# A state-space and gated feed-forward backward kernel: w1 and w3 are transposed through DRAM during the gradient pass instead of at the start of the input-gradient pass

## The chip, the cores and the metric

The kernel runs on one core of a Trainium2 chip. The metric is the device time of one execution in microseconds (us). Before the change it is 2046.6 us, the median of 7 runs (2042.9 to 2064.46). The core has five engines that work side by side, each through a queue of its own in program order: TensorE (PE, matmuls; PEld are its weight loads), VectorE (DVE), ScalarE (ACT), GpSimd (POOL) and SyncE (SP). SP, ACT and POOL also issue DMA transfers, which 16 DMA engines carry out; SPq and ACTq are these issues in the profile. SBUF is the on-chip memory of 128 partitions, PSUM holds matmul results, DRAM is the memory beside the core.

## The reference, cut to what matters

The forward pass normalizes `u` (2048 x 576), sends it through a diagonal state-space convolution (`_A_ref`, 128 states) and through a gated feed-forward block of width 4608, and multiplies the two. The kernel returns the output and the gradients of `u`, of the eight state-space parameters and of the three weights.

```python
def _B_ref(x, w1, w3, w2):
    gate = jnp.einsum("bsd,df->bsf", x, w1)
    up = jnp.einsum("bsd,df->bsf", x, w3)
    h = _silu(gate) * up
    out = jnp.einsum("bsf,fd->bsd", h, w2)
    return out
...
xn = _layernorm(x, axis=-1)
s = _A_ref(xn, A_A_re, A_A_im, A_B_re, A_B_im, A_C_re, A_C_im, A_log_dt, A_Dskip)
g = _silu(_B_ref(xn, B_w1, B_w3, B_w2))
return x + s * g
```

The part that the change concerns is the gradient of `xn` through the feed-forward block: with GG the gradient of `gate` and GU that of `up` (both 2048 x 4608), it is GG times w1 transposed plus GU times w3 transposed. TensorE needs GG, GU, w1 and w3 with the 4608 axis on the partitions for that, so all four are transposed on the way into SBUF.

## The kernel before, in words

The forward part (lines 86 to 837) ends near 790 us of the span. What follows is `backward`, line 1066, and three strands of work share the engines in it.

**The gradient pass** goes over the 4608 axis in 18 groups of 256 (`FG`). `phase6_load` fetches a group ahead of time: two blocks of w2 through row tiles `w2r` (POOL, line 1139) and transposed on SP into `w2T` (lines 1140 and 1123), the stored gate and up values `gg_n` and `h_n` (POOL, lines 1144 and 1145), and their silu and its derivative (ACT, DVE, lines 1149 to 1154). `phase6_group` computes the gradient of h (matmuls into `ph`, line 1172, from `goT` and `w2T`; ACT casts it to `gh`, line 1175), multiplies it into `gu_n` and `gg_n` (DVE, line 1178), writes these to GU_dram and GG_dram (SP, line 1185), and forms the gradients of w2 (line 1200, from `go_o` and `h_n`) and of w1 and w3 (lines 1219 to 1227, then ACT casts `gw`, lines 1204, 1221 and 1230, and writes on ACT's queue, lines 1205, 1222, 1231 and 1232). `go_o` and the four `goT` tiles stay in SBUF through the pass.

**The state-space gradient** runs beside it: first `conv_bwd_quarter` four times (lines 866 to 948), which ends each quarter by writing 16 pieces of its gradient of `xn` to GXN_dram in fp32 on ACT's queue (line 948), then 36 chunks of `param_quarter` (lines 950 to 980). A chunk loads `gz` (SP, line 959), `qT` by a transposing DMA on SP (lines 962 and 1123) and `pz` (ACT's queue, line 964), multiplies on TensorE into `et_ps` (line 970) and reduces on DVE (lines 977 and 979). The last chunks run beside the next pass; `phase5_final` (lines 982 to 1062) turns their sums into the parameter gradients, with `load_rates` ahead of it.

**The input-gradient pass**, `phase6_inputs`, line 1234, goes over 16 tiles of 128 rows. For a tile, SP loads `ggc` and `guc` (128 x 36 x 128 each) by transposing DMAs from GG_dram and GU_dram (lines 1248 and 1249), with two buffers each; TensorE runs 144 matmuls of 288 columns into `px` (line 1262) over 36 blocks; DVE adds the piece of GXN_dram (`gxs`, line 1255) into `gx` (line 1265), and `ln_bwd_tile` applies the layernorm's gradient and writes `out_1`.

The transposed weights are two sets of tiles. Blocks 0 to 11 of w1 and w3 (`FA = 12`) are loaded by ten transposing DMAs in the gradient pass (line 1097). Blocks 12 to 35 are loaded by ten more in the pool `x_wB`, inside the second pass behind the `ggc` and `guc` of tile 0 (line 1251): the pool lies over the memory of the gradient pass.

The order of each queue is not written out by hand. `self.at(us)` sets the priority of what is traced after it, as a due time (T0 = 560, 36 us for a group, T2 = 1208 for the second pass, 18 us for a tile of it, 15 us for a chunk), and the tile framework orders each engine's instructions by it, allots the slots of each pool and adds the waits. A tile that takes a slot waits for everything that used the slot before. An engine that waits holds all that stands behind in its queue.

Of the kernel before, what the change touches and what calls it, by code (L numbers as in the profile page):

```python
# [11 lines left out]
ALU = mybir.AluOpType  # L12
AX = mybir.AxisListType
FP32 = mybir.dt.float32
BF16 = mybir.dt.bfloat16
I32 = mybir.dt.int32
P = 128
# [43 lines left out]
class K:  # L61
# [669 lines left out]
    def forward_tail(self, T0, TB, TQ, gctx):  # L731
        nc, cfg = self.nc, self.cfg
# [3 lines left out]
        W = D // 4  # L736
# [8 lines left out]
        PS = bass.MemoryType.PSUM  # L745
        gop = gctx.enter_context(pool(name="go_keep", bufs=1))
        self.go_o = gop.tile([P, LT, D], BF16, name="go_o")
# [3 lines left out]
        with pool(name="g_all", bufs=1, side="right") as gp, pool(name="o_ep", bufs=3, side="right") as ep, \  # L751
# [9 lines left out]
            with pool(name="o_ep1", bufs=1) as ep1, pool(name="o_h", bufs=2) as hp, \  # L761
# [41 lines left out]
                for g in range(3):  # L803
                    quarter(g)
            gtp = gctx.enter_context(pool(name="go_t", bufs=1))
            self.goT += [gtp.tile([P, DT, KT * P], BF16, name=f"goT{m}") for m in range(NB // 2, NB)]
# [59 lines left out]
    def conv_bwd_quarter(self, g, kp, zp, ps, T0, TQ):  # L866
# [68 lines left out]
        for j in range(NB):  # L935
# [7 lines left out]
            for oc in range(KT):  # L943
# [3 lines left out]
                nc.vector.tensor_tensor(out=gx[:, oc, :], in0=pt[:, 0:W], in1=gx[:, oc, :], op=ALU.add)  # L947
            nc.scalar.dma_start(out=self.GXN_dram[:, j * KT:(j + 1) * KT, cs], in_=gx[:])

    def param_quarter(self, g, gz, S_all, qp, ps, T0, TC):  # L950
# [3 lines left out]
        for cc in range(NQ):  # L954
# [8 lines left out]
            pz = qp.tile([P, 3, 16, AV], BF16, name="pz")  # L963
            nc.scalar.dma_start(out=pz[:], in_=self.PZ_dram[:, ch])
            for h in range(2):
# [100 lines left out]
    def backward(self, T0, TG, TQ, TC, TX, gctx, mats):  # L1066
# [6 lines left out]
        T2 = T0 + TG * NG  # L1073
        FA = 12
        pool = self.tc.tile_pool
        PS = bass.MemoryType.PSUM
        with ExitStack() as out:
            ffn = ExitStack()
            wp = ffn.enter_context(pool(name="e_w", bufs=2))
            elp = ffn.enter_context(pool(name="e_el", bufs=3))  # L1080
            gwp = ffn.enter_context(pool(name="e_gw", bufs=2))
            rowp = ffn.enter_context(pool(name="e_w2r", bufs=1))
            inp = ffn.enter_context(pool(name="e_in", bufs=2))
            self.at(T0 - TG)
# [11 lines left out]
            self.at(T2 - 150)  # L1096
            wT = [self.load_wT(wA, 0, FA)]
            T1 = T0 + 4 * TQ
# [4 lines left out]
            for gi in range(NG):  # L1103
                nxt = self.phase6_load(gi + 1, T0 + TG * gi, TG, wp, inp) if gi + 1 < NG else None
                self.at(T0 + TG * gi)
                self.phase6_group(gi, cur, elp, gwp, ps_h, ps_gw)
                cur = nxt
            ffn.close()
            gctx.close()
            self.phase6_inputs(T2, TX, FA, wT)  # L1110

    def load_wT(self, pool, f0, f1):
        cfg = self.cfg
        tiles = []
        for w in ("B_w1", "B_w3"):
            t = pool.tile([P, f1 - f0, cfg.D], BF16, name=f"wT{w}{f0}")
            for (do, dsz) in cfg.dch:
                self.nat_transpose(t[:, :, do:do + dsz], self.aps[w][do:do + dsz, f0 * P:f1 * P])
            tiles.append(t)
        return tiles  # L1120

# [3 lines left out]
    def phase6_load(self, gi, T, TG, wp, inp):  # L1125
# [8 lines left out]
        LH = LT // 2  # L1134
        w2T = wp.tile([P, nfl, DT, P], BF16, name="w2T")
        for fl in range(nfl):
            fi = gi * nfl + fl
            w2r = self.w2rows[fi % len(self.w2rows)]
            nc.gpsimd.dma_start(out=w2r[:, 0:D], in_=aps["B_w2"][fi * P:(fi + 1) * P, :])
            self.nat_transpose(w2T[:, fl], w2r[:])  # L1140
        gg = inp.tile([P, LT, FG], BF16, name="gg_n")
        hn = inp.tile([P, LT, FG], BF16, name="h_n")
# [90 lines left out]

    def phase6_inputs(self, T2, TX, FA, wT):
        nc, cfg = self.nc, self.cfg
        D, DT, L, LT, F, FT = cfg.D, cfg.DT, cfg.L, cfg.LT, cfg.F, cfg.FT
        aps = self.aps
        pieces = self.dpieces()
        with self.tc.tile_pool(name="x_wB", bufs=1) as wB, \
                self.tc.tile_pool(name="x_in", bufs=2) as inp, \  # L1240
                self.tc.tile_pool(name="l_sb", bufs=2) as sb, self.tc.tile_pool(name="l_sm", bufs=4) as sm, \
                self.tc.tile_pool(name="x_ps", bufs=2, space=bass.MemoryType.PSUM) as ps:
            for i in range(LT):
                self.at(T2 + TX * i)
                if True:
                    ggc = inp.tile([P, FT, P], BF16, name="ggc")
                    guc = inp.tile([P, FT, P], BF16, name="guc")
                    self.nat_transpose(ggc[:], self.GG_dram[i])
                    self.nat_transpose(guc[:], self.GU_dram[i])
                    if i == 0:  # L1250
                        wT = wT + [self.load_wT(wB, FA, FT)]
                    px = [ps.tile([P, 512], FP32, name=f"px{pi_}") for pi_ in range(len(pieces))]
                    gx = sb.tile([P, D], FP32, name="gx7")
                    gxs = sb.tile([P, D], FP32, name="gxs7")
                    nc.scalar.dma_start(out=gxs[:], in_=self.GXN_dram[:, i, :])
                    go_t = sb.tile([P, D], BF16, name="go7")
                    nc.scalar.dma_start(out=go_t[:], in_=aps["grad_out"].flatten_outer_dims()[i * P:(i + 1) * P, :])
                    for fi in range(FT):
                        part, f = (0, fi) if fi < FA else (1, fi - FA)
                        for ai, act in enumerate((ggc, guc)):  # L1260
                            for pi_, (po, pw) in enumerate(pieces):
                                nc.tensor.matmul(px[pi_][:, 0:pw], lhsT=act[:, fi, :], rhs=wT[part][ai][:, f, po:po + pw],  # L1262
                                                 start=(fi == 0 and ai == 0), stop=(fi == FT - 1 and ai == 1))
                    for pi_, (po, pw) in enumerate(pieces):
                        nc.vector.tensor_tensor(out=gx[:, po:po + pw].rearrange("p (g d) -> p g d", g=4),  # L1265
                                                in0=px[pi_][:, 0:pw].rearrange("p (g d) -> p g d", g=4),
                                                in1=self.perm(gxs[:])[:, :, pi_, :], op=ALU.add)
                    self.ln_bwd_tile(sb, sm, gx, i, go_t)

    def ln_bwd_tile(self, sb, sm, gx, i, go_t):  # L1270
# [8 lines left out]
        nc.scalar.activation(out=t[:], in_=g, func=ACT.Copy, scale=-invD, accum_out=mg[:])  # L1279
        t2 = sb.tile([P, D], BF16, name="t27")  # L1280
        mgx = sm.tile([P, 1], FP32, name="mgx")
        nc.vector.tensor_tensor_reduce(out=t2[:], in0=g, in1=xh, scale=1.0, scalar=0.0, op0=ALU.mult,  # L1282
                                       op1=ALU.add, accum_out=mgx[:])
# [5 lines left out]
        nc.vector.tensor_tensor(out=u[:], in0=g, in1=t[:], op=ALU.add)  # L1289
        o1 = sb.tile([P, D], BF16, name="o1")  # L1290
        nc.vector.scalar_tensor_tensor(out=o1[:], in0=u[:], scalar=self.rstd[:, i:i + 1], in1=go_t[:],
# [96 lines left out]
```

## Time and profile before

| | us |
|---|---|
| median of 7 runs (lowest to highest) | 2046.6 (2042.9 to 2064.46) |
| the profiled execution | 2050.35 |
| its span, first to last instruction | 2048.6 |
| last matmul of the gradient pass starts | 1636.2 |
| first and last matmul of the input-gradient pass start | 1653.1, 2008.7 |
| mean granted TensorE clock, share of full speed | 0.949 |
| transposing DMAs of w1 and w3 on SP: count, median time of one issue | 20, 2.97 |
| transposing DMAs of ggc and of guc: count each, median issue | 16, 5.68 and 6.06 |
| transposing DMAs of qT, of w2T: count each, median issue | 36, 3.70 and 1.23 |

How to read it: a page of the profile gives the busy time of each engine, its share of slices of the span, and groups of instructions by line. A row of a timeline has its start, its length, the engine, the line, the operation, and what it writes and reads (`out<-in`). A wait is named by what ended it. A DMA issue takes time on the queue that issues it, and the data lands later. The DMA share is the mean busy share of the 16 DMA engines; it counts overlapping packets, so it can exceed 1.

### The profile page before, as it was taken

What the parts mean: (1) busy time and instruction counts of PE and PEld (TensorE: products, weight loads), DVE (VectorE), ACT (ScalarE), POOL (GpSimd) and SP (SyncE); (2) the same over time, 40 slices, a digit from 0 to 9 for tenths busy, and PEclk for the clock granted to TensorE, in tenths of its full rate; (3) what the DMA queues carried; (4) which work ended last, traced back from release to release, by engine and by line L of the source; (5) the groups of instructions that cost most, each with busy time, mean ns of one, the idle gap of its engine ahead of it and who ended that gap; (6) DMA issues with size and microseconds to landing.
All of it is one profiled execution on the core that took longest, in us unless ns stands there. A gap on an engine that the chain in (4) does not pass through costs nothing. (4 is left out here: it accounts for less than half of the span.)

```text
span 2048.6 us, 41825 instructions
## 1 busy us (share of the span) xinstructions
PE 1764.7 (86%) x17174; PEld 1292.5 (63%) x17174; DVE 1429.3 (70%) x2772; ACT 992.4 (48%) x1668; POOL 248.6 (12%) x324
## 2 busy tenths in 40 slices
PE   2889999999699995989899998888988938999892
PEld 1534444444488874777777777777777826777681
DVE  7538888888387723685874868666977555768567
ACT  2778888888445545765646656444454200000000
POOL 4003333333312102000000000100000000000000
PEclk9999999999899997999999999999999959999996
DMA  3578888896956568465473655898879499999981
GB/s 84 200 285 305 306 296 300 289 320 250 304 142 175 137 139 263 130 173 168 141 200 113 175 166 157 220 238 212 223 183 218 127 229 215 217 234 196 212 162 22
DMA packets 615087, 416.04 MB, mean 203 GB/s; under 512 B 403184, under 2 KB 560752, under 8 KB 610288
## 3 DMA queue, kind: packets, MB, share of 16 engines
q1 hardware_dynamic: 539632, 264.00, 53.0%
q0 software_dynamic: 23056, 105.00, 14.6%
q10 hardware_dynamic: 52208, 44.37, 8.1%
q8 instruction: 134, 2.20, 0.4%
q14 instruction: 57, 0.47, 0.1%
HBM read 133.01 MB, written 188.01 MB: 157 GB/s over the span
## 5 line engine op out<-in xcount | busy, mean ns | idle before, releaser
L719 PE MATMUL pgu<-wmB_w,xnT 128*128 128x512 bf16 x1152 | 284.1, 382 | 1.1 <-ACT E_k L392 1.1
L1262 PE MATMUL px<-wTB_w,guc 128*128 128x288 bf16 x1152 | 242.4, 291 | 24.2 <-DMA guc<-GU_dram 12.2
L1262 PE MATMUL px<-wTB_w,ggc 128*128 128x288 bf16 x1152 | 244.3, 291 | 20.7 <-DMA ggc<-GG_dram 11.3
L977 DVE TENSOR_TENSOR pr_q<-et_ps,pz 128x512 f32<-128x512 f32 x288 | 186.5, 680 | 92.5 <-PE et_ps L970 92.5
L1219 PEld LDWEIGHTS <-xn_bf 128*128 128x128 bf16 x2304 | 225.0, 98 | 34.5 <-issue 7.6
L1172 PE MATMUL ph<-w2T,goT 128*128 128x256 bf16 x1440 | 194.1, 284 | 32.1 <-ACT gh L1175 30.1
L719 PEld LDWEIGHTS <-xnT 128*128 128x128 bf16 x1152 | 103.5, 98 | 125.2 <-issue 20.9
L1172 PEld LDWEIGHTS <-goT 128*128 128x128 bf16 x1440 | 142.4, 102 | 54.7 <-issue 30.3
L1279 ACT ACTIVATE t<-gx 128x576 f32<-128x576 f32 x16 | 10.9, 683 | 342.1 <-DVE gx L1265 320.6
L979 DVE TENSOR_REDUCE S_all<-pr_q 128x16 f32<-128x1024 f32 x144 | 173.8, 1210 | 0.5
L1200 PE MATMUL pgw<-go_o,h_n 128*128 128x288 bf16 x1152 | 162.2, 296 | 8.4 <-DVE h_n L1154 8.4
L784 PE MATMUL po<-w2g,hc 128*128 128x288 bf16 x1152 | 148.8, 286 | 2.9 <-DMA hc<-H_dram 2.9
L1221 ACT CAST gw<-pgw 128x256 bf16<-128x256 f32 x144 | 54.0, 377 | 199.8 <-PE pgw L1219 195.1
L1262 PEld LDWEIGHTS <-guc 128*128 128x128 bf16 x1152 | 113.8, 99 | 55.6 <-DMA guc<-GU_dram 13.3
L1262 PEld LDWEIGHTS <-ggc 128*128 128x128 bf16 x1152 | 113.3, 99 | 50.4 <-DMA wTB_w<-in_B_w_dram 9.0
L1200 PEld LDWEIGHTS <-h_n 128*128 128x128 bf16 x1152 | 115.4, 101 | 41.3 <-DVE h_n L1154 8.9
L1219 PE MATMUL pgw<-gu_n,xn_bf 128*128 128x256 bf16 x1152 | 131.7, 272 | 3.7 <-ACT gw L1221 1.7
L784 PEld LDWEIGHTS <-hc 128*128 128x128 bf16 x1152 | 111.4, 98 | 30.5 <-DMA hc<-H_dram 3.4
L1219 PE MATMUL pgw<-gg_n,xn_bf 128*128 128x256 bf16 x1152 | 128.9, 273 | 0.8 <-ACT gw L1221 0.8
L1175 ACT CAST gh<-ph 128x512 bf16<-128x512 f32 x144 | 84.3, 618 | 71.3 <-PE ph L1172 34.4
L1178 DVE TENSOR_TENSOR gu_n<-gh,gu_n 128x1024 bf16<-128x1024 bf16 x72 | 49.3, 685 | 97.9 <-ACT gh L1175 97.7
L722 ACT ACTIVATE s_t<-pgu 128x512 bf16<-128x512 f32 x144 | 87.4, 608 | 54.2 <-PE pgu L721 53.9
(301 smaller groups left out, 3622.7 us busy)
## 6 DMA issues: line engine op xcount, KB each, us to landing
GI_dram<-gu_t POOLq DMA_DIRECT2D x72, 512.0 KB, 5.7
H_dram<-h_t SPq DMA_DIRECT2D x72, 256.0 KB, 5.3
Q_dram<-q_k SPq DMA_DIRECT2D x36, 512.0 KB, 5.3
gg_n<-GI_dram POOLq DMA_DIRECT2D x18, 1024.0 KB, 6.0
h_n<-GI_dram POOLq DMA_DIRECT2D x18, 1024.0 KB, 8.8
GU_dram<-gu_n SPq DMA_DIRECT2D x36, 512.0 KB, 3.8
GG_dram<-gg_n SPq DMA_DIRECT2D x36, 512.0 KB, 7.2
E_dram<-E_k SPq DMA_DIRECT2D x18, 768.0 KB, 3.7
```

What stands on the lines that cost most here:

```text
L719: nc.tensor.matmul(pgu[:, j], lhsT=xnT[:, c, ts], rhs=wm[w][:, c, :], start=(c == 0), stop=False)
L722: nc.scalar.activation(out=s_t[:, :, q, :], in_=pgu[:, 0].rearrange("p (g f) -> p g f", g=ng), func=ACT.Silu)
L784: nc.tensor.matmul(pos[k][:, pi_, 0:pw], lhsT=hcs[k][:, fi, :], rhs=w2[fi][:, po:po + pw], start=(fi == 0), stop=(fi == FT - 1))
L977: nc.vector.tensor_tensor(out=pr[:, r], in0=T[r][:], in1=pz[:, s + r, h * 8:h * 8 + 8, :][:, :, None, :] .to_broadcast([P, 8, 2, AV]), op= ...
L979: nc.vector.tensor_reduce(out=S_all[:, 2 * s:2 * s + 2, d0:d0 + 8].rearrange("p k d -> p d k"), in_=pr[:].rearrange("p r d k a -> p d k r ...
L1172: nc.tensor.matmul(ph[j][:, k, :].rearrange("p (a f) -> p a f", f=P), lhsT=lw, rhs=rh, start=(n == 0), stop=(n == nfull))
L1175: nc.scalar.copy(out=gh[:, j], in_=ph[j][:])
L1178: nc.vector.tensor_tensor(out=t_[:, sl], in0=gh[:].rearrange("p j t f -> p (j t) f"), in1=t_[:, sl], op=ALU.mult)
L1200: nc.tensor.matmul(pgw[pi_][:, 0:pw], lhsT=hn[:, tt, fl * P:(fl + 1) * P], rhs=go_o[:, tt, po:po + pw], start=(tt == 0), stop=(tt == LT - 1))
L1219: nc.tensor.matmul(pw_[:, 0:FG], lhsT=self.xn_bf[:, tt, c * P:(c + 1) * P], rhs=nat[:, tt, :], start=(tt == 0), stop=(tt == LT - 1))
L1221: nc.scalar.copy(out=gw[:, c, :], in_=pw_[:, 0:FG])
L1262: nc.tensor.matmul(px[pi_][:, 0:pw], lhsT=act[:, fi, :], rhs=wT[part][ai][:, f, po:po + pw], start=(fi == 0 and ai == 0), stop=(fi == FT - ...
```

## The change

Blocks 12 to 35 of w1 and w3 are transposed three blocks at a time during the gradient pass. For each of groups 0 to 15, `prep_wT` fills a tile by five transposing DMAs on SP and writes it out to a new tensor WT_dram on POOL's queue. The tile takes a slot of `w2T`, whose pool goes from 2 to 3 buffers and whose slots grow to 3 x 576 elements. In the last group `late_wT` loads 20 blocks (10 of each weight) from WT_dram, without transposing, into the `gg_n`, `h_n` and `gu_n` slots that group 16 has left; 16 more go into the four `goT` tiles once the last `ph` matmuls are done, and the last 12 into the pool `x_wB`. All these loads are on SP.

The second pass gets no pool of its own for `ggc` and `guc`. Even tiles use the memory of `go_o`, odd ones the `gg_n`, `gu_n` and `h_n` slots of group 17, where each of the two operands is split into 32 and 4 blocks, so an odd tile has four transposing DMAs. Those of tile 0 are issued before the pass: 34 blocks early, the two of the last group after it.

Besides: GXN_dram is written in the natural order of its columns, so that the add in the second pass reads and writes plain rows in place, by two DMAs on SP in place of one on ACT; `pz` is loaded on SP in place of ACT; two scratch tiles of the layernorm go. The order of the pools changes, since the pool of `gg_n`, `h_n` and `gu_n` must outlive the gradient pass.

```diff
-            nc.scalar.dma_start(out=self.GXN_dram[:, j * KT:(j + 1) * KT, cs], in_=gx[:])
+            for h in range(2):
+                nc.sync.dma_start(out=self.GXN_dram[:, j * KT:(j + 1) * KT, :].rearrange(
+                    "p t (h g d) -> p t h g d", h=2, g=4)[:, :, h, g], in_=gx[:, :, h * W // 2:(h + 1) * W // 2])
...
-            nc.scalar.dma_start(out=pz[:], in_=self.PZ_dram[:, ch])
+            nc.sync.dma_start(out=pz[:], in_=self.PZ_dram[:, ch])
...
-            wp = ffn.enter_context(pool(name="e_w", bufs=2))
+            inp = gctx.enter_context(pool(name="e_in", bufs=2))
             elp = ffn.enter_context(pool(name="e_el", bufs=3))
+            wp = ffn.enter_context(pool(name="e_w", bufs=3))
+            rowp = ffn.enter_context(pool(name="e_w2r", bufs=1))
             gwp = ffn.enter_context(pool(name="e_gw", bufs=2))
-            rowp = ffn.enter_context(pool(name="e_w2r", bufs=1))
-            inp = ffn.enter_context(pool(name="e_in", bufs=2))
...
             self.at(T2 - 150)
-            wT = [self.load_wT(wA, 0, FA)]
+            wT = [[None] * FT, [None] * FT]
+            self.load_wT(wA, 0, FA, wT)
...
+                if gi == NG - 1:
+                    self.at(T0 + TG * gi)
+                    self.late_wT(inp, FA, wT)
...
+    def prep_wT(self, pool, k, FA):
+        cfg = self.cfg
+        FT, D = cfg.FT, cfg.D
+        n = 3
...
+        f, ai = FA + k // 2 * n, k % 2
+        if f >= FT:
+            return
+        t = pool.tile([P, n, D], BF16, name="w2T")
+        for (do, dsz) in cfg.dch:
+            self.nat_transpose(t[:, :, do:do + dsz],
+                               self.aps[("B_w1", "B_w3")[ai]][do:do + dsz, f * P:(f + n) * P])
+        self.nc.gpsimd.dma_start(out=self.WT_dram[ai, :, f:f + n, :], in_=t[:])
+
+    def wT_into(self, dst, ai, f0, wT):
+        n = dst.shape[1]
+        if f0 == 0:
+            for (do, dsz) in self.cfg.dch:
+                self.nat_transpose(dst[:, :, do:do + dsz], self.aps[("B_w1", "B_w3")[ai]][do:do + dsz, 0:n * P])
+        else:
+            self.nc.sync.dma_start(out=dst, in_=self.WT_dram[ai, :, f0:f0 + n, :])
+        for f in range(n):
+            wT[ai][f0 + f] = dst[:, f, :]
...
+        self.at(T + 0.5 * TG)
+        self.prep_wT(wp, gi, self.FA)
+        self.at(T)
...
+            self.at(T2 - 0.5 * TG)
+            gts = []
+            for m in range(4):
+                t = (self.gop if m < 2 else self.gtp).tile([P, DT, self.cfg.KT * P], BF16, name=f"goT{m}")
+                n = DT * self.cfg.KT * P // D
+                gts.append(t[:].rearrange("p c t -> p (c t)")[:, 0:n * D].rearrange("p (r d) -> p r d", d=D))
+            for ai in range(2):
+                for j in range(2):
+                    self.wT_into(gts[2 * ai + j], ai, self.fl + n * j, wT)
...
+            sets = [[[(0, FT, even[:, ai])] for ai in range(2)],
+                    [[(0, FL, odd[ai]), (FL, FT, odd[2][:, ai * (FT - FL):(ai + 1) * (FT - FL)])] for ai in range(2)]]
+            FN = FT - self.FG // P
+            for ai, src in enumerate((self.GG_dram, self.GU_dram)):
+                self.nat_transpose(even[:, ai, 0:FN], src[0, :, 0:FN * P])
+            self.load_wT(wB, fl, FT, wT)
+            self.at(T2 - 0.3 * TG)
+            for ai, src in enumerate((self.GG_dram, self.GU_dram)):
+                self.nat_transpose(even[:, ai, FN:FT], src[0, :, FN * P:FT * P])
...
-                    ggc = inp.tile([P, FT, P], BF16, name="ggc")
-                    guc = inp.tile([P, FT, P], BF16, name="guc")
-                    self.nat_transpose(ggc[:], self.GG_dram[i])
-                    self.nat_transpose(guc[:], self.GU_dram[i])
-                    if i == 0:
-                        wT = wT + [self.load_wT(wB, FA, FT)]
+                    parts = sets[i % 2]
+                    if i > 0:
+                        for ai, src in enumerate((self.GG_dram, self.GU_dram)):
+                            for (a, b, t) in parts[ai]:
+                                self.nat_transpose(t[:, 0:b - a], src[i, :, a * P:b * P])
...
-                        nc.vector.tensor_tensor(out=gx[:, po:po + pw].rearrange("p (g d) -> p g d", g=4),
-                                                in0=px[pi_][:, 0:pw].rearrange("p (g d) -> p g d", g=4),
-                                                in1=self.perm(gxs[:])[:, :, pi_, :], op=ALU.add)
-                    self.ln_bwd_tile(sb, sm, gx, i, go_t)
+                        nc.vector.tensor_tensor(out=gxs[:, po:po + pw], in0=px[pi_][:, 0:pw], in1=gxs[:, po:po + pw],
+                                                op=ALU.add)
+                    self.ln_bwd_tile(sb, sm, gxs, i, go_t)
```

## The prediction

> **What bounds the kernel now.** I read the busy shares first, then the slices, then the stretch where the slices of TensorE dip, and there the queue of SyncE (SP), which issues every transposing DMA. The first line says that TensorE is the busiest engine over the whole span; the three stretches under it (start:end, length, busy us of each engine, then granted clock, DMA share, GB/s) say that one stretch is different.
>
> ```profile
> PE 1764.7 (86%) x17174; PEld 1292.5 (63%) x17174; DVE 1429.3 (70%) x2772; ACT 992.4 (48%) x1668; POOL 248.6 (12%) x324
> ```
> ```profile
> 1590.00:1637.00 47.00, 46.88 (x492) 40.51 (x490) 24.52 (x36) 11.93 (x29) 0.00 (x0) 1.00 0.45 127
> 1637.00:1712.00 75.00, 31.47 (x259) 22.16 (x259) 36.70 (x51) 0.78 (x2) 0.00 (x0) 0.66 1.12 222
> 1712.00:1769.00 57.00, 56.84 (x537) 45.32 (x536) 33.42 (x54) 2.33 (x6) 0.00 (x0) 1.00 1.14 221
> ```
>
> In the last gradient group (to 1637) TensorE is full and the DMA engines are less than half used; then for 75 us TensorE works 31.5 us, at a granted clock of 0.66, while the DMA share stands at 1.12; after that TensorE is full again, with the DMA share no lower. The SP timeline says what fills the gap:
>
> ```profile
> 1642.37 5.67 SPq L1123 DMA_TRANSPOSE ggc<-GG_dram  x1
> 1648.09 6.26 SPq L1123 DMA_TRANSPOSE guc<-GU_dram  x1
> 1654.40 35.15 SPq L1123 DMA_TRANSPOSE wTB_w<-in_B_w_dram  x10
> ...
> 1693.08 4.91 SPq L1123 DMA_TRANSPOSE ggc<-GG_dram  x1
> 1698.03 5.57 SPq L1123 DMA_TRANSPOSE guc<-GU_dram  x1
> ```
>
> Ten transposes of w1 and w3 (two thirds of them, 2x576x3072x2 B = 7.08 MB) take SP 35.15 us, 201 GB/s, ahead of tile 1's own transposes. Nothing before 1637 covers them. Tile 0's result is taken from PSUM at 1701.6, tile 1's at 1727.9, and tile 13's at 1970.0 (starts of the L1265 rows): 242.1/12 = 20.2 us a tile in the steady pass.
>
> **Part 1, the ten transposes leave the second pass.** TensorE's account: tile 0 needs go_o free (last L1200 matmul ends 1620.1), so its transposes can enter SP behind the last group's GU/GG writes (issued to 1621.3). Two big ones at the medians 5.7 us issue and 10 us to landing: 1621.3+5.7+10 = 1637. The last two blocks wait for the last GG write (1620+7.2) and then for the big ones on SP; by the small w2T transposes (1.23 us issue, 2.6 us landing) 1633+2.5+2.6 = 1638. Six plain loads (four into the goT tiles, two into wB) may stand ahead or behind at 0.5 us each. So tile 0 can begin near 1641 instead of ending at 1701.6; one steady tile of 18.8 us (spacing of tiles 1 to 3) ends at 1660, 42 us earlier. Tile 1 came 26.3 us after tile 0 and would come 20.2 after: 6 us more. **Saving by TensorE: 48 us.** Behind tile 13 the tail (SP loads the rates behind the last guc, then phase5_final on DVE, then tile 15's layernorm, 78.6 us from 1970.0 to the end) keeps its order and shifts with it.
>
> The DMA engines' account is smaller. The 7.08 MB do not vanish from this stretch: they come back as plain loads, late_wT 2.95 MB in the last group, goT 2.36 and wB 1.77 MB at the boundary. At the best slice of the page, 320 GB/s, they take 22 us, at 222 GB/s 32 us; take 24, so 35-24 = 11 us are saved. The rest must come from the unused DMA of the last group: from 1602, when the tiles of group 16 are free, to 1637 the share is 0.53 against 1.12, (1.12-0.53)/1.12 x 35 = 18 us. **Saving by DMA: 30 us.** Which one counts depends on whether the pass is bound by TensorE or by DMA, and it is nearly both: a tile asks for 4.4 MB (ggc and guc 2.36, 1.2 chunks of qT, pz and gz at 1.18, gxs, go and o 0.59), at 221 GB/s 19.7 us, between the 18.8 of a full TensorE and the 20.2 on average. I take the middle, **39 us**, ends 30 and 48.
>
> **Part 2, the toll in the gradient pass (790 to 1637).** Added: 16 blocks of 5 transposes on SP, 16 writes of 442 KB on POOL. Nearest row from below: the 36 small w2T transposes held TensorE for 2.0 us in all (its waits), 0.056 us each, 80 x 0.056 = 4.5 us. Nearest row from above, the first third of w1 and w3, ten transposes in the same pass:
>
> ```profile
> 1309.00:1362.00 53.00, 41.27 (x410) 34.40 (x408) 28.57 (x44) 19.83 (x33) 6.92 (x7) 0.92 1.11 252
> ```
>
> TensorE is at 41.3 of 53 us where the rest of the stage has 89% (290.7 of 327): 5.8 us lost for 3.54 MB, so 12 us for 7.08 MB. DMA has room: the share is 0.58 from 790 to 1310, which leaves 251 us of full use; transposes 32 us plus the extra write and its load. SP itself: 5 x 1.23 = 6.2 us a group of 47 us, with waits of tens of us in it now. A prep tile takes the slot of the group's own w2T, so it waits for the last ph matmul (L1172), as the next w2T does today (126.4 us of SP waiting); behind it stand the GU/GG writes, qT and gz. The WT_dram write on POOL waits for its transposes; behind it stand w2r, gg_n and h_n of a later group, which today wait for the end of L1227 anyway. **I take 8 us**, the middle of 4.5 and 12.
>
> **Part 3, the moves between queues.** GXN writes: 16 of ACT become 32 on SP with pieces of 288 B instead of 576. DVE waits for them today 12.3 us in 4 waits (gx L941); doubled, +12.3; below, 0; I take 3, since most are not waited for. pz goes from ACT to SP, 36 x 0.33 us; in front of ACT's casts stand waits for DVE that fit it (gh after pr_q and S_all, 3.8+2.4 us), so up to -6 us, and on SP pz waits for DVE with ggc behind it; I take -2 in the gradient pass. The odd tiles' splits are 2 more small transposes in 8 tiles, 2 x 1.23 x 8 = 20 us of SP, hidden while DMA and not SP is the limit; without that cover half of it would be late. The add in natural order and o1 as scratch replace rows of 0.45 and 0.74 us by equal ones: 0. Toll of parts 2 and 3: 8+3-2 = 9 us, ends -30 (all the time that TensorE's ph waits for gh goes) and +86 (below).
>
> A rule against part 3: the Trainium skill, "DMA: Bandwidth & Descriptors", Specifications, wants at least 512 B per piece for full rate, and 288 B lies below it where 576 did not. The trace shows 576 B pieces landing in 3.0 us (median); no run here shows 288 B. If each of 16 landings doubled by that rule and DVE waited for all, the sum would be 48 us worse; by the trace's own waits it is the 0 to 12 above.
> A second: the same page, Rules for kernel authors, calls transfers under 64 KB mostly overhead. The 64-row pieces here are 48 KB, the others 96 KB; the smallest transposes of the trace are the 160 KB w2T. If these 80 paid 2 us each by that rule, SP would carry 160 us more over 16 groups, still inside its waits.
>
> **Sum.** Profiled execution: span 2048.6, time 2050.35, so 1.75 us lie around it; it is 3.75 us over the median of the seven runs, 2046.6, and I carry the difference over. -39+9 = -30: 2050.35-30 = 2020.4, and against the median 2046.6-30 = **2016.6 us**.
>
> **Rivals.**
> *DMA keeps all of it* (chance 0.2): the pass is DMA-bound throughout, the saving is 30, the toll at 12+12 = 24: -6, **2040.6**. For: share 1.14 to 1.19 to the end, late guc at 1902 and 1974. Against: TensorE 56.84 of 57 us.
> *TensorE's account is right and the queues get lighter* (0.2): -48 and the toll 0 or below: -48 to -62, **1998** or less. For: the waits on ACT that may go.
> *ACT is held by SP's transposes, slower* (0.13). Writes on ACT's queue were held until a transpose on SP landed:
> ```profile
> ACT gh L1175 <- DMA qT<-Q_dram: 16.2, 3, 8.3
> ```
> (gh's waits: total, times, longest), 5.4 us each; at 1576.31 the write of gw2 goes out as qT lands, 15.9 us after its issue. If each of 16 prep blocks does it once, 16 x 5.4 = 86 us and the sum is -39+86 = +47, **2094**; it decides from 39/16 = 2.4 us per block. Half of it, +4, is 2051. Against: small transposes land in 2.6 us, qT in 6.2.
> *The gap stays* (0.07): tile 0's transposes are queued behind late loads and the stall takes another name: **2046**.
>
> Chances: forecast 0.4 (2005 to 2030). Range: 0.1 off each end, 1990 to 2052. A measurement here tells about 0.5%, 10 us, from no change: faster 0.4+0.2+0.07 (a third of the first rival) = 0.67, same 0.20, slower 0.13.
>
> **What would show it.** Right: TensorE at 90% or more from 1637 on, clock 1.0 instead of 0.66; no wB transposes between tiles 0 and 1; the first DVE reads of px, against the end of the gradient pass, about 42 us earlier for tile 0 and 30 to 48 for tile 13; DMA share in the last group near 1; gradient pass 0 to 20 us longer. Part 2 wrong: waits of gh or gw for a DMA of w2T (the prep tiles), or of ph for gh, well over 30 us. Part 1 wrong: a new wait of px for goT, wB or ggc, or tiles over 21 us apart.

## The result and the profile after

The changed kernel takes **2080.97 us**, the median of 12 runs (2063.02 to 2091.5), against 2046.93 for the kernel before beside it (31 runs): a ratio of **1.0151, 95% interval 1.0126 to 1.0176**. It is slower by 34 us where 30 us less was forecast. Its profiled execution took 2076.51 us with a span of 2074.7; the kernel before had 2050.35 and 2048.6, so the two traces differ by 26.1 us in the span.

Where the 26.1 us lie is read from one row, the last `gwt` cast of ACT, which ends the gradient pass: 1636.53 before, 1710.70 after. **The gradient pass ends 74.2 us later; what follows it is 48.1 us shorter** (412.1 us before, 364.0 after). Stretches of the profile after (start:end, length, busy us of PE, PEld, DVE, ACT, POOL, then granted clock, DMA share, GB/s); the first is the end of the gradient pass, the other two begin where it ends:

```profile
1680.00:1710.70 30.70, 30.62 (x302) 26.33 (x300) 14.20 (x21) 7.84 (x19) 0.00 (x0) 1.00 1.11 288
1710.70:1785.70 75.00, 60.42 (x574) 46.64 (x574) 53.97 (x76) 1.92 (x5) 0.00 (x0) 0.93 1.14 240
1785.70:1842.70 57.00, 55.63 (x544) 43.68 (x542) 47.67 (x72) 2.33 (x6) 0.00 (x0) 1.00 1.14 230
```

The gap is gone: in the 75 us where TensorE worked 31.5 us at a clock of 0.66 it now works 60.4 at 0.93. The toll is in the pass ahead of it. The same stretch in both kernels, from 790 us to the end of the pass, before and after:

```profile
790.00:1636.53 846.53, 750.88 (x7650) 636.45 (x7651) 603.76 (x1095) 457.04 (x949) 42.46 (x72) 0.96 0.68 183
```
```profile
790.00:1710.70 920.70, 776.09 (x7690) 652.59 (x7688) 609.02 (x1104) 461.56 (x956) 50.86 (x86) 0.93 0.72 189
```

TensorE does the same work: 750.9 x 0.96 = 721 against 776.1 x 0.93 = 722. So 25 us of the 74 are longer matmuls at a lower granted clock and 49 us are idle time. Group by group (the `gwt` cast of each of the 18) the lag grows: 17 us at group 0, 27 at group 1, 32 at group 4, 46 at group 9, 80 at group 13, and 74 at the end. The waits say what holds it. ACT waiting for gg_n between 780 and 1720 us (total, times, longest), before and then after:

```profile
ACT gu_n L1149 <- DMA gg_n<-GI_dram: 9.1, 6, 2.3
ACT L1149 <- DMA gg_n<-GI_dram: 1.0, 2, 0.7
```
```profile
ACT L1193 <- DMA gg_n<-GI_dram: 76.3, 11, 13.1
ACT gu_n L1193 <- DMA gg_n<-GI_dram: 1.2, 1, 1.2
PE ph L1216 <- ACT gh L1219: 60.2, 20, 8.9
```

ACT's wait for gg_n went from 10.1 us to 77.5, and TensorE's own wait for `gh`, which ACT casts, went from 30.1 to 60.2. One group shows how. The timelines of POOL, SP and ACT of the kernel after, around the end of a group at 1494.72:

```profile
1493.87 0.55 POOL L1137 DMA_DIRECT2D WT_dram<-w2T  x1 [14.75 <-DMA w2T<-in_B_w_dram]
1501.16 0.54 POOL L1180 DMA_DIRECT2D w2r<-in_B_w_dram  x1 [6.74 <-DMA w2T<-w2r]
1502.47 0.54 POOL L1180 DMA_DIRECT2D w2r<-in_B_w_dram  x1 [0.76 <-DMA w2T<-w2r]
1503.05 0.54 POOL L1188 DMA_DIRECT2D gg_n<-GI_dram  x1
```
```profile
1482.14 9.79 SPq L1163 DMA_TRANSPOSE w2T<-in_B_w_dram  x3
1498.02 2.52 SPq L1163 DMA_TRANSPOSE w2T<-w2r  x2
```
```profile
1494.72 0.37 ACT L1274 CAST gwt<-pgw 128x256 bf16<-128x256 f32 x1 [1.53 <-PE pgw L1271]
1497.77 0.58 ACT L1219 CAST gh<-ph 128x512 bf16<-128x512 f32 x1 [0.34 <-PE ph L1216]
1511.44 1.28 ACT L1193 ACT_TABLE_LOAD   x1 [13.09 <-DMA gg_n<-GI_dram]
```
```profile
1514.31 1.65 PE L1216 MATMUL ph<-w2T,goT 128*128 128x256 bf16 x7 [8.88 <-ACT gh L1219]
```

The buffer of gg_n is free when the group ends, 1494.72. But POOL stands first before the write of the prep block (its transposes took 9.79 us for three of the five issues), then before two `w2r` loads, whose row tiles the `w2T` transposes must have read; these in turn stand on SP until the block's write has freed their slot. gg_n goes out at 1503.05, ACT's silu starts at 1511.44, and ACT does nothing for 13.09 us while TensorE waits 8.88 us for the `gh` behind it. Before, POOL stood at gg_n itself and let it go as the group ended at 1477.00; the `w2r` ahead of it had gone out 20 us earlier:

```profile
1477.23 0.53 POOL L1144 DMA_DIRECT2D gg_n<-GI_dram  x1 [19.41 <-PE pgw L1227]
1496.18 0.53 POOL L1145 DMA_DIRECT2D h_n<-GI_dram  x1 [18.42 <-PE pgw L1200]
```

### The profile page after: what moved, and what is told of

The parts are those of the page before. It is cut to its first block, busy times and chain, and to the rows that moved or that the text cites. A ratio compares the mean times of both kernels' runs of the same rounds, so it can differ in the third digit from the quotient of the medians.

```text
span 2074.7 us, 42081 instructions
## 1 busy us (share of the span) xinstructions
PE 1782.1 (86%) x17174; PEld 1303.2 (63%) x17174; DVE 1429.2 (69%) x2772; ACT 992.3 (48%) x1668; POOL 264.5 (13%) x340
## 5 line engine op out<-in xcount | busy, mean ns | idle before, releaser
L1216 PE MATMUL ph<-w2T,goT 128*128 128x256 bf16 x1440 | 200.8, 290 | 62.9 <-ACT gh L1219 60.2
L784 PE MATMUL po<-w2g,hc 128*128 128x288 bf16 x1152 | 153.9, 292 | 16.2 <-DMA hc<-H_dram 16.2
L1343 ACT ACTIVATE t<-gxs 128x576 f32<-128x576 f32 x16 | 10.9, 683 | 296.6 <-DVE gxs L1330 296.6
L1327 PEld LDWEIGHTS <-go_o 128*128 128x128 bf16 x1152 | 111.8, 99 | 38.4 <-DMA go_o<-GU_dram 6.4
L582 PEld LDWEIGHTS <-dSi 128*128 128x128 bf16 x768 | 76.4, 100 | 41.9 <-issue 41.0
L467 DVE TENSOR_SCALAR m_k<-et_ps 128x512 int32<-128x512 int32 x108 | 73.7, 682 | 33.0 <-PE et_ps L466 32.7
L728 POOL DMA_DIRECT2D GI_dram<-gu_t x72 | 68.5, 952 | 216.3 <-DVE gu_t L724 110.2
```

The source lines that it names most:

```text
L467: nc.vector.tensor_scalar(out=m[:, o:o + 512], in0=pt[:].bitcast(I32), scalar1=15, scalar2=15, op0=ALU.logical_shift_left, op1=ALU.arith_s ...
L582: nc.tensor.matmul(pv, lhsT=mat[:, kt, sl], rhs=V[:, :, ri, kt, :], start=(i == 0), stop=(i == n - 1))
L784: nc.tensor.matmul(pos[k][:, pi_, 0:pw], lhsT=hcs[k][:, fi, :], rhs=w2[fi][:, po:po + pw], start=(fi == 0), stop=(fi == FT - 1))
L1216: nc.tensor.matmul(ph[j][:, k, :].rearrange("p (a f) -> p a f", f=P), lhsT=lw, rhs=rh, start=(n == 0), stop=(n == nfull))
L1327: nc.tensor.matmul(px[pi_][:, 0:pw], lhsT=act, rhs=wT[ai][fi][:, po:po + pw], start=(fi == 0 and ai == 0), stop=(fi == FT - 1 and ai == 1))
```

## The experiments

Ratios are to the kernel before, run on the same chip in the same session, with 95% intervals. Runs of one kernel scatter by 10 to 30 us, so differences under some 8 us between medians are not told apart. Theory A: the toll is the prep blocks, through the order of the queues. Rival C: it is the transfers moved between queues. A second rival, B, came up on the way: it is the DMA work of the blocks, their traffic or the transposes as such.

**No blocks at all.** Left out: the 16 blocks; the late loads read rows of w2, so the gradient of `u` is another.

```diff
-        self.at(T + 0.5 * TG)
-        self.prep_wT(wp, gi, self.FA)
-        self.at(T)
...
-            self.nc.sync.dma_start(out=dst, in_=self.WT_dram[ai, :, f0:f0 + n, :])
+            self.nc.sync.dma_start(out=dst, in_=self.aps["B_w2"][f0 * P:(f0 + n) * P, :].rearrange("(r p) d -> p r d", p=P))
```

> The change without its prep blocks: no transposes of w1 and w3 in the groups and no writes to the scratch tensor; the late loads read rows of w2 of the same shape instead, so the input gradient is computed from w2 in place of blocks 12 to 35 of w1 and w3. Everything else stays: pool order, three w2T buffers, GXN writes and pz on SP, the second pass without transposed weights. Theory A (the toll is the prep blocks): the gradient pass, which ends at 1636.5 us before and 1710.7 after, ends at 1635 to 1655, and the time is 1998 to 2020. Theory C (the toll is the reordering of the pass by the moved GXN and pz transfers and the pools): the pass still ends past 1690 and the time is 2055 or more.

Measured: 2004.26 us, ratio 0.9778 (0.9718 to 0.9838). The stretch from 790 us to the end of the pass is 4.5 us longer than before, and ACT waits 11.4 us for gg_n:

```profile
790.00:1641.03 851.03, 754.11 (x7665) 639.10 (x7665) 607.26 (x1103) 459.73 (x956) 41.86 (x71) 0.96 0.70 191
```

What follows the pass takes 364.5 us, as in the changed kernel. So everything else that the change does is worth 43 us, and the blocks cost 2081 - 2004 = **77 us**. Rival C is out. Against the kernel before this pass is 12.6 us late at group 0 and 4.5 at its end, so the lag that grows through the pass comes from the blocks.

**Transposes without the writes.** The WT_dram write is left out too, the blocks are transposed and not kept.

```diff
-        self.nc.gpsimd.dma_start(out=self.WT_dram[ai, :, f:f + n, :], in_=t[:])
```

> As the first, but the 80 small transposes stay and only the 16 writes on POOL's queue go; the late loads again read w2, so the input gradient is computed from w2 in place of blocks 12 to 35 of w1 and w3. Theory A1 (POOL's write, which waits for its transposes, holds back the next group's gg_n load, ACT stands before silu with the gh casts behind it): ACT's wait for gg_n falls from 76 us to under 20, the pass ends at 1640 to 1665, time 2000 to 2030. Theory B (the transposes themselves, by SP's queue and the DMA engines): the pass ends past 1690, time 2055 or more.

Measured: 2048.81 us, 1.0017 (0.9984 to 1.005), between the two ranges: ACT still waits 32.1 us for gg_n and the pass ends at 1681.9. Taken in this order, the transposes bring 45 of the 77 us and the writes on top of them 32. With no write in its queue POOL still has `w2r` ahead of gg_n; the last cast of the group starts at 1481.89:

```profile
1482.29 0.54 POOL L1179 DMA_DIRECT2D w2r<-in_B_w_dram  x1 [17.53 <-DMA w2T<-w2r]
1485.24 0.54 POOL L1179 DMA_DIRECT2D w2r<-in_B_w_dram  x1 [2.41 <-DMA w2T<-w2r]
1485.83 0.53 POOL L1187 DMA_DIRECT2D gg_n<-GI_dram  x1
```

**The write on SP instead of POOL.**

```diff
-        self.nc.gpsimd.dma_start(out=self.WT_dram[ai, :, f:f + n, :], in_=t[:])
+        self.nc.sync.dma_start(out=self.WT_dram[ai, :, f:f + n, :], in_=t[:])
```

> The change with the 16 writes to the scratch tensor issued on SP instead of POOL; TensorE's and ACT's orders are the same as in the change. On POOL the next gg_n then stands behind two w2r loads only, which wait for w2T. Theory A1 in its short form (the write alone): ACT's wait for gg_n under 25 us, the pass ends at 1650 to 1675, time 2015 to 2040. Theory A2 (the chain write, w2T slot, w2r, gg_n): w2T still takes the slot that the write frees, so only part comes back: the pass ends at 1680 to 1705, time 2045 to 2070. Theory B: 2075 or more, since SP has more to do.

Measured: 2074.09 us, 1.0132 (1.0075 to 1.019), not told apart from the changed kernel. The ranges of A1 and A2 are both missed, and it is 1 us short of that of theory B. ACT's wait for gg_n falls from 77.5 to 47.2 us, yet the pass ends at 1710.2 as in the changed kernel. So the write's place on POOL was not the toll by itself; that the wait only moved to SP's queue is the reading, and it is not shown.

**gg_n on ACT's queue.**

```diff
-        nc.gpsimd.dma_start(out=gg[:], in_=self.GI_dram[gi, :, 0])
+        nc.scalar.dma_start(out=gg[:], in_=self.GI_dram[gi, :, 0])
```

> The change with one line altered: the 18 loads of gg_n are issued on ACT's queue, so nothing of POOL stands ahead of them. Theory A1 or A2: the loads go out within 1 us of the group's end, ACT's wait for gg_n falls under 30 us, the pass ends at 1650 to 1680 and the time is 2015 to 2045. Theory B: no change, 2070 or more.

Measured: 2040.82 us, 0.9948 (0.9908 to 0.9989). **One line gives 40 of the 77 us back.** ACT's own queue reaches the load as the group ends, so nothing that is due earlier stands behind it; the wait for gg_n is 17.2 us in the pass:

```profile
1480.56 0.34 ACTq L1188 DMA_DIRECT2D gg_n<-GI_dram  x1
1480.94 0.37 ACT L1274 CAST gwt<-pgw 128x256 bf16<-128x256 f32 x1 [1.88 <-PE et_ps L972]
...
1486.53 1.28 ACT L1193 ACT_TABLE_LOAD   x1 [0.22 <-DMA gg_n<-GI_dram]
```

**The side moves alone**: the kernel before with GXN's writes and pz on SP (the first two parts of the diff of the change) and the add in natural order.

```diff
-                        nc.vector.tensor_tensor(out=gx[:, po:po + pw].rearrange("p (g d) -> p g d", g=4),
-                                                in0=px[pi_][:, 0:pw].rearrange("p (g d) -> p g d", g=4),
-                                                in1=self.perm(gxs[:])[:, :, pi_, :], op=ALU.add)
+                        nc.vector.tensor_tensor(out=gx[:, po:po + pw], in0=px[pi_][:, 0:pw], in1=gxs[:, po:po + pw],
+                                                op=ALU.add)
```

> The kernel before with only the side moves: each GXN write as two on SP with half-length pieces, pz on SP, the add of the second pass in natural order. Theory A (the toll comes from the prep blocks, in the queues): these moves are cheap, about the 4.5 us by which the gradient pass of the kernel without preps was longer; 2042 to 2056 us, point 2050. Rival C (the moved transfers are the toll): 2075 or more, with DVE waiting for gx or PE for qT over 30 us more than before.

Measured: 2023.38 us, 0.9881 (0.9845 to 0.9917). Neither theory had this: the moves do not cost, they give 24 us. Two runs later split it (below).

**The blocks two loads later**: none is issued ahead of the forward's last `hc` transposes.

```diff
-        self.prep_wT(wp, gi, self.FA)
+        self.prep_wT(wp, gi - 2, self.FA)
...
-        if f >= FT:
+        if k < 0 or f >= FT:
```

> The changed kernel, but the first prep block is issued with the load of group 2 instead of group 0, so that no prep block stands in SP's queue ahead of the hc transposes of the forward's end; the last of the 16 goes out with the load of group 17. POOL's order (w2r, w2r, gg_n) stays. Theory A: only the early part of the toll comes back, that is the 12 us by which group 0 to 4 of the changed kernel lie behind those of the kernel without preps; 2062 to 2074 us, point 2068, and ACT still waits 60 us or more for gg_n. If the early blocks cost nothing: 2081. If the whole toll came from them: below 2040.

Measured: 2073.55 us, 1.014 (1.0079 to 1.0201). Group 0's lag falls from 16.8 to 6.8 us and group 9's from 46.1 to 34.5, but at the end it is 69.2 against 74.2, which the scatter covers; ACT waits 81.4 us for gg_n, both inside what theory A expected. The early blocks are not the toll.

**Both edits, and with h_n on ACT as well**, two kernels; the second has this line more:

```diff
-        nc.gpsimd.dma_start(out=hn[:], in_=self.GI_dram[gi, :, 1])
+        nc.scalar.dma_start(out=hn[:], in_=self.GI_dram[gi, :, 1])
```

> Both edits: gg_n's load on ACT's queue and the prep blocks two loads later. Theory A (queue order): the two costs lie in different places, so both come back; 2040.8 less 8 to 16, 2025 to 2033 us, point 2029; group 0 ends 10 us or more earlier than with gg_n on ACT alone. Rival B (what is left of the toll is DMA traffic: 21 MB more in the pass, TensorE's clock): the place of the blocks does not matter, 2036 to 2044.

> As the one before, and h_n's load on ACT's queue too, so that POOL issues only w2r and the writes of the transposed blocks, and nothing that the gradient group reads waits behind them. Theory A: up to the 14 us that TensorE still waited for h_n with gg_n alone on ACT, and no more: 0 to 10 us under the run before it, 2018 to 2030, point 2024. Rival B: no gain, within 3 us of it; slower than it if ACT now waits for h_n's buffer ahead of its casts.

Measured: 2041.34 us, 0.9968 (0.9935 to 1.0), and 2046.21 us, 1.0 (0.9966 to 1.0034). Theory A failed here twice: the first result is in rival B's range, the second 5 us slower still, which the scatter covers. The two edits do not add up, and taking the last load of a group off POOL gives nothing: ACT's wait for gg_n is 9.3 and 8.0 us, as before the change, yet 37 us of the toll stay (2041 - 2004, medians). The first kernel's trace is of its fastest execution, 2026.34 us, 19 above that of the kernel without blocks, so its waits show only about half of these 37. With h_n on ACT TensorE waits 24.9 us for ACT's `gw` casts instead.

**What the 37 us hang on.** Three kernels, each that with gg_n on ACT and late blocks and one more edit. The first leaves out the write (the late loads read w2). The second keeps the write and fills a block by one plain load of w2 rows, so its second pass has other numbers:

```diff
-        for (do, dsz) in cfg.dch:
-            self.nat_transpose(t[:, :, do:do + dsz],
-                               self.aps[("B_w1", "B_w3")[ai]][do:do + dsz, f * P:(f + n) * P])
+        self.nc.sync.dma_start(out=t[:], in_=self.aps["B_w2"][f * P:(f + n) * P, :].rearrange("(r p) d -> p r d", p=P))
```

The third does the whole work, with the blocks in a buffer of their own, each released behind the first quarter silu of a load; gg_n is on ACT from group 2 on:

```diff
-            wp = ffn.enter_context(pool(name="e_w", bufs=3))
+            wp = ffn.enter_context(pool(name="e_w", bufs=2))
+            pp = self.prepp = ffn.enter_context(pool(name="e_p", bufs=1))
...
-        t = pool.tile([P, n, D], BF16, name="w2T")
+        t = pool.tile([P, n, D], BF16, name="w13T")
+        self.nc.scalar.copy(out=t[0:1, 0, 0:D:P], in_=after[0:1, 0, 0:5])
...
             nc.scalar.activation(out=gu[:, sl, :], in_=gg[:, sl, :], func=ACT.Silu)
+        if gi >= 2:
+            self.prep_wT(self.prepp, gi - 2, self.FA, gu)
```

> Measured so far: 2004 us with no prep blocks, 2041 with gg_n on ACT and the blocks two loads later; 37 us of toll are still open. This kernel is the latter without the writes of the blocks; the transposes stay, and the late loads read rows of w2 instead, so the two gradients that the second pass makes are not the reference's. Theory S (what is left is the slot chain: w2T and prep tiles alternate in three buffers, and SP stands before a buffer): a buffer is free as soon as its transposes have landed, so most of it goes: 2008 to 2025 us, point 2018. Theory B (what is left is the transposes' own DMA work): 2034 to 2044.

> gg_n on ACT, blocks two loads later, writes kept, but each block is brought in by one plain load of w2 rows (442 KB) instead of five transposes, so the second pass computes with other numbers than the reference. The buffers and the waits for them stay. Theory S: the chain is the same, 2034 to 2044 us. Theory B (transposing costs, not the bytes): the toll goes, 2005 to 2020. Point 2030.

> The whole work, with the prep blocks in a buffer of their own (w2T has its two again), each block's transposes released by a five-element copy on ACT behind the first quarter silu of the load, first block with the load of group 2, gg_n on ACT from group 2 on. Theory S: SP never stands before a buffer that TensorE or the block's write holds: 2006 to 2022 us, point 2015, under the 2023 of the moves alone. Theory B: 2034 to 2044.

Measured: without the write 2017.55 us, 0.9834 (0.9784 to 0.9885); plain load 2001.38, 0.9754 (0.9709 to 0.9798); own buffer 2020.97, 0.9858 (0.9801 to 0.9914). So 24, 40 and 20 of the 37 us go. Theory B is wrong in the first and third run, theory S in the second: the slots count (own buffer), and the transposes count although slots and writes stay (plain load). The third run changes three things at once, though: the blocks' buffer, the two slots of `w2T` and the moment a block is released. The plain load moves the same 442 KB (the DMA share of the pass is 0.76 in both), so it is not the bytes. The pass in the kernel with transposes and in that with plain loads:

```profile
790.00:1661.26 871.26, 752.31 (x7652) 638.31 (x7651) 609.08 (x1102) 457.37 (x953) 39.99 (x67) 0.94 0.76 202
```
```profile
790.00:1630.17 840.17, 745.80 (x7643) 633.90 (x7643) 606.00 (x1099) 458.33 (x954) 40.03 (x67) 0.96 0.76 208
```

What differs is the time that a block holds SP and its buffer: five issues of 1.25 us (median; up to 6.8) and 2.7 us to landing, against one of 0.39 (up to 3.6) and 3.5. The chain is slot, transposes, landing, write, slot, `w2T`: whole it costs 37 us, some 13 to 17 without the write or with a slot of its own, and nothing when its longest link, the transposes, is short. That reading fits the three runs, but it is argued: no single wait of TensorE carries the 37 us.

**Own buffer, gg_n left on POOL**, and the same with the write on SP behind the group's GU/GG writes:

```diff
-        self.nc.gpsimd.dma_start(out=self.WT_dram[ai, :, f:f + n, :], in_=t[:])
+        self.pend = (self.WT_dram[ai, :, f:f + n, :], t)
...
                 nc.sync.dma_start(out=dst[ts, :, gi * FG:(gi + 1) * FG].rearrange("t p f -> p t f"), in_=t_[:, ts, :])
+        if self.pend:
+            nc.sync.dma_start(out=self.pend[0], in_=self.pend[1][:])
+            self.pend = None
```

> As the run before it, but gg_n stays on POOL, where it is now again ahead of the two w2r of its load as in the kernel before. Theory A with S (what hurt was gg_n behind w2r, w2T and their buffers): within 10 us of the run before it, 2008 to 2030, ACT waits for gg_n under 25 us. If any wait of POOL for a block's transposes hurts gg_n: 2050 or more, with 50 us of ACT waiting for gg_n.

> The whole work, blocks in a buffer of their own and released as in the two runs with that, gg_n on POOL, and the block's write on SP behind the group's GU/GG writes, so that POOL issues w2r, gg_n and h_n alone, as in the kernel before. If POOL's wait for the block was what lay between 2021 (gg_n on ACT) and 2034 (on POOL): 2010 to 2024 us, point 2018. If SP's wait for the landing costs as much: 2030 to 2040.

Measured: 2034.42 us, 0.9918 (0.9879 to 0.9957), and 2037.86 us, 0.9945 (0.9914 to 0.9976). The first is above its range, though ACT's wait for gg_n, 22.5 us, is as expected; the second is in the range of the alternative. In the second POOL issues nothing of the blocks, and ACT still waits 46.2 us for gg_n. In the two longest of its seven waits, 27.5 us of the 46.2, a `w2r` ahead of gg_n has waited for `w2T` on SP, where a block and its write stand ahead. In one of them, with the group's last cast at 1416.01:

```profile
1409.71 2.81 SPq L1232 DMA_DIRECT2D WT_dram<-w13T  x1
1412.58 6.10 SPq L1166 DMA_TRANSPOSE w2T<-w2r  x1
```
```profile
1424.37 0.54 POOL L1182 DMA_DIRECT2D w2r<-in_B_w_dram  x1 [16.07 <-DMA w2T<-w2r]
1424.98 0.54 POOL L1187 DMA_DIRECT2D gg_n<-GI_dram  x1
```
```profile
1432.56 1.28 ACT L1192 ACT_TABLE_LOAD   x1 [12.63 <-DMA gg_n<-GI_dram]
```
```profile
ACT L1192 <- DMA gg_n<-GI_dram: 46.2, 7, 14.9
```

In the longest wait, 14.9 us, gg_n went out only 3 us after the group's last cast, and the load itself took 15.5 us to land.

**Plain loads in the changed kernel itself**, gg_n on POOL, everything else as changed.

> The changed kernel with one edit: each block comes in by one plain load of w2 rows instead of five transposes, so the second pass computes with other numbers than the reference. gg_n on POOL, the three shared buffers, the order of issue by the same rule and the write stay. If gg_n's place behind w2r and the buffers costs by itself: 2030 to 2045 us, with 50 us or more of ACT waiting for gg_n. If the chain only costs through the length of the transposes (6 us of SP for a block, then the landing): 2000 to 2012, gg_n waits near 10. Point 2010.

Measured: 2028.15 us, 0.9922 (0.9884 to 0.996), between the two theories, with ACT waiting 30.1 us for gg_n. With it the toll can be laid out in a square (medians; no blocks: 2004; the 2001 has its blocks two loads later, which made no difference to the 2041):

| | gg_n on POOL | gg_n on ACT |
|---|---|---|
| transposed blocks | 2081 | 2041 |
| plain blocks | 2028 | 2001 |

gg_n's place costs 27 us without the transposes and 40 with them; the transposes cost 40 us without gg_n's place and 53 with it. So the shares depend on the order in which they are taken: the blocks with gg_n on POOL cost 24 us even when nothing is transposed.

**pz alone, and GXN with the add alone**, each on the kernel before; the first is this line, the second the rest of the side moves.

```diff
-            nc.scalar.dma_start(out=pz[:], in_=self.PZ_dram[:, ch])
+            nc.sync.dma_start(out=pz[:], in_=self.PZ_dram[:, ch])
```

> The kernel before with pz's load on SP instead of ACT, nothing else. If the 24 us of the side moves come from ACT no longer standing before pz's buffer with its casts behind it: 2020 to 2030 us, point 2025. If they come from GXN's writes and the add: 2042 to 2050.

> The kernel before with GXN's writes as two half-length pieces on SP and the add in natural order; pz stays on ACT. If pz is the cause: 2040 to 2050 us. If GXN is: 2022 to 2030. By the prediction's own term it would lose 3: 2050.

Measured: pz 2025.98 us, **0.9906 (0.9868 to 0.9944)**; GXN and the add 2054.03 us, 1.0013 (0.9977 to 1.0048). pz is the cause: 19 us by the ratio. A place where the two kernels differ is ACT's timeline in the kernel before, at group 16: `gw` is cast, its write issues 9 us later, as a transpose of qT on SP ends, and `gh` behind it is as late.

```profile
1566.84 0.68 ACT L1204 CAST gw<-pgw 128x288 bf16<-128x288 f32 x2
1567.40 1.07 ACT L1149 ACTIVATE gu_n<-gg_n 128x1024 bf16<-128x1024 bf16 x1
1576.31 0.38 ACTq L1205 DMA_DIRECT2D out_dram<-gw  x1
1576.73 1.07 ACT L1175 CAST gh<-ph 128x512 bf16<-128x512 f32 x2 [8.26 <-DMA qT<-Q_dram]
```
```profile
1567.38 8.89 SPq L1123 DMA_TRANSPOSE qT<-Q_dram  x1
```

With pz on SP the write follows the cast at once; the three waits of `gh` for qT (16.2 us in all) are gone in that kernel and in that with all the moves, and 11.1 us of them stay where only GXN was moved. No load of pz issues on ACT between 1562.32 and 1576.31, so how its place there holds a later write is not shown:

```profile
1567.59 0.68 ACT L1204 CAST gw<-pgw 128x288 bf16<-128x288 f32 x2
1568.16 1.07 ACT L1151 ACTIVATE gg_n<-gg_n 128x1024 bf16<-128x1024 bf16 x1
1568.30 0.35 ACTq L1205 DMA_DIRECT2D out_dram<-gw  x1
```

The kernels that do the whole work and are fastest are the own buffer with gg_n on ACT (2021), the moves alone (2023) and pz alone (2026); the runs do not tell them apart.

## Why the prediction was wrong, point by point

**The failed step** is this one of part 2: "The WT_dram write on POOL waits for its transposes; behind it stand w2r, gg_n and h_n of a later group, which today wait for the end of L1227 anyway." It took for granted that gg_n would still be issued when L1227 ends. In the trace of before only gg_n waits for that; the `w2r` wait for `w2T` on SP, and had gone out 11 to 26 us before the group's end. With the blocks SP is late with `w2T`, the second `w2r` goes out after the group's end in 11 of 13 groups, and gg_n goes out 3 to 11 us after it in 10 of 16. The step beside it, "SP itself: 5 x 1.23 = 6.2 us a group of 47 us, with waits of tens of us in it now", failed too, since SP's waits were not free time: what stood behind them came late. **Toll of part 2: 8 taken, 4.5 to 12 as the ends, 77 measured.** The upper end came from ten transposes whose results nothing in the pass waits for, so it priced their DMA and not their place in a queue. (Its 89% also counted the slow 53 us themselves; the other 275 us are at 91%, which makes it 14 instead of 12.)

**Part 1** was right for the second pass, and short of an entry for the first. What follows the gradient pass is 48.1 us shorter, TensorE's account (48); the first read of px comes 37.1 us after the end of the pass instead of 65.1, so 28 earlier and not 42, and tile 13 at 1998.65, 45.4 us earlier, inside the 30 to 48. The rest is the tail. Two corrections: about 10 us of this stretch came with the side moves alone (401.9 us after the pass against 412.1, one trace each), and the kernel without blocks has a gradient pass 14.6 us longer than that with the moves alone (1641.0 against 1626.4), an entry that the sum did not have. By medians the step from the moves alone to no blocks is worth 19 us (2023 to 2004), where 39 was taken. Of these 14.6 us, 6.5 are there at group 0, where six `w2T` transposes that the third buffer lets go early stand ahead of four `hc` transposes (TensorE waits 11.3 us for hc, against 1.1 with the moves alone).

**Part 3**: GXN +3, pz -2, add 0, so +1 was taken; measured -24 (pz 19, GXN and add nothing that can be told). The "up to -6 us" was read from waits of `gh` for DVE (pr_q and S_all), and these stayed with pz on SP: 7.1 us in place of 6.2. What went are the 16.2 us of `gh` waiting for qT, which the prediction showed in a fence for another purpose. The rule on pieces under 512 B that was weighed there would have made it 48 us worse; with GXN moved alone the half-length pieces of 288 B landed in 2.8 us (median; 4.3 in the changed kernel) against 3.0 for the whole ones, and that kernel is at 1.0013. The 2 us for each small transfer were counted as time of SP; the 80 transposes issue in 1.25 us (median), and only the 16 of 48 KB are under the 64 KB of that rule.

**The rivals.** That on the slower side named ACT held by SP's transposes, 2094, at 86 us of toll. That its time is near is luck. The sign of part 2 being wrong ("ph for gh, well over 30 us") came, 60.2 us, but not by this rival's mechanism: ACT waits behind a DMA of `w2T` twice, 6.7 and 0.8 us, and is held by a load that comes late from POOL. The rival on the faster side was right that the queues get lighter (the 24 us of the moves), but took the toll for nothing. "DMA keeps all of it" is out (TensorE's account holds at a DMA share of 1.14), and the gap did not stay.

**Ledger by medians**: moves -24, the rest of the change without blocks -19, transposes +45, writes +32, sum +34, as measured. The sum took -39 for the second of these and +9 for the others together. What stays open is how the 37 us that are left with gg_n on ACT divide between SP's time and the chain of buffers: each edit that was tried takes 20 to 40 of them.

## What to carry to other kernels

A load that an engine has been waiting on punctually is punctual because of what stands ahead of it: before work is put into a queue with waits of tens of us, list for each load behind it which event releases it today, and price the work as a delay of that event and not as use of idle time. A load that gates an engine is worth trying on the queue that reaches that point of the program by itself, as gg_n on ACT was (40 us for one line). Try each side move of a change alone: here pz, for which the plan had 2 us, gave 19, and no kernel that does the whole work was told apart from it on the faster side.

## What the runs showed of the hardware

Here 36 loads of pz that issue in 0.33 us each (median; 12 us in all) gave 19 us when they went from ACT to SP, and 18 loads of gg_n (0.54 us each on POOL, 10 us in all) gave 40 when they went from POOL to ACT. So what moves with a DMA is more than its issue time: the wait in front of it and all that stands behind move too. The Trainium skill, "Trainium Kernel Development and Optimization", Key Constraints, says that issuing DMAs from several engines only saves the sequencer's issue time, as they share the DMA engines; these two runs do not agree.

Longer passes ran at a lower granted clock. From 790 us to the end of the pass, it is 0.96 to 0.97 in the kernels where that takes 829 to 851 us (pz alone, moves alone, plain blocks with gg_n on ACT, GXN and the add alone, before, no blocks), 0.94 to 0.95 from 858 to 890, and 0.92 to 0.93 where it takes 892 to 921 (no write, blocks two loads later, write on SP, the change). With 49 us more of idle time spread over the pass, TensorE's unchanged work took 25 us longer, a third of the toll. That the idle time is what lowers the clock is the reading; no run sets one without the other.
